# A two-layer SiLU kernel on one core: the first 512 rows computed contraction tile by contraction tile, with x loaded in columns

## The chip, the cores and the metric

The kernel runs on one core of a Trainium2 chip. The metric is device time in microseconds (us), from the kernel's start to its end on that core. A profile is one execution recorded instruction by instruction; its span runs from the first to the last recorded instruction, and the execution's own time is a little longer.

## The reference

```python
x:  (1, 2048, 640) bf16      w1: (640, 1728) bf16      w2: (1728, 640) bf16

h = jnp.einsum("bsd,df->bsf", x, w1)
h = _silu(h)                                   # h * sigmoid(h)
out = jnp.einsum("bsf,fd->bsd", h, w2)
```

So: 2048 rows; a first product that contracts over D = 640, an activation, and a second product that contracts over F = 1728.

## The kernel before

**Tiles.** The 2048 rows are four chunks of SCH = 512 rows (`sc`). D is five contraction tiles of 128 (`dt`), F is thirteen tiles of 128 (`ft`, FR = 13) and a last one of 64. The first product is computed transposed: for one `ft` and one chunk a *unit* (lines 205 to 213) runs five matmuls over `dt` into one of the eight PSUM banks. Each has a 128x128 block of w1 as its loaded weights and 512 columns of the transposed x, `xT_sb[:, dt, cols]`, as the moving operand. `silu` (lines 190 to 203) then lets ScalarE (ACT) write the sigmoid of the bank to `sig_sb` (L193) and VectorE (DVE) multiply the two into `hT_sb` (L196), after which the bank is free. `take_bank` hands the banks out in rotation. The 64 last columns of w1 are done for two chunks at once (`tail_unit`, L219), and the second product follows (L289 and after).

**Order.** A small planner lists operations in program order for each engine, and emits semaphore waits for what each operation depends on. Nothing is reordered: each engine, and each of the two DMA queues in use (SP's and ACT's), runs its list from front to back, and a wait holds up all that stands behind it on that engine.

**The start.** The changed part is the work on the first chunk:

- SP issues rows 0 to 127 and 256 to 383 of x, ACT rows 128 to 255 and 384 to 511, each 128 rows by 640 columns, 160 KB (`load_x0`, L145).
- ACT then issues the first two 128-column pieces of w1, all five contraction tiles of each (`load_w1`, L150). SP waits until its second piece of x has landed, and issues the columns 256 to 511, 512 to 1023 and 1024 to 1727 of w1.
- TensorE (PE) runs six matmuls on constants (L158), five with 512 columns and one with 256, which read nothing that is loaded.
- For each of the four 128-row pieces of x, PE runs five 128x128 transposes (L167) into two banks; DVE copies three of the five to `xT_sb` (L173), ACT the other two (L175).
- `ft` 0 and 1 are computed in two halves of 256 rows each (L209), so that the first two units need only the first two pieces of x. `ft` 2 to 12 take 512 rows a unit.

The transposed x of the other three chunks comes from transposing DMAs (L231), five a chunk, which SP issues after its loads of w1; the first of them waits for the last but one of those loads (`w1_dma[-2]`). Between the second and the third of these chunks SP issues w2 as well. In the rest of the program the order of the work is not touched.

Of the kernel before, what the change touches and what calls it, by code (L numbers as in the profile page):

```python
# [20 lines left out]
class Plan:  # L21
# [9 lines left out]
    def add(self, eng, emit, deps=(), group=None):  # L31
        op = Op(eng, emit, [d for d in deps if d is not None], group)
        self.ops.append(op)
        return op
# [40 lines left out]
def bass_standalone__dense_activation_silu__prompt_kernel(  # L75
# [6 lines left out]
    bf16 = mybir.dt.bfloat16  # L82
# [5 lines left out]
    F = w1.shape[1]  # L88
    P = 128
    H = P // 2  # L90
    SCH = 512
    DT = D // P
    FR = F // P
    F_LAST = F - FR * P
    FT = FR + 1
    ST = S // P
    NSC = S // SCH
    JB = SCH // P
    NBANK = 8
    TPV = 3  # L100
    assert D % P == 0 and S % (2 * SCH) == 0 and F_LAST == H and D == 640

    with ExitStack() as es:
        def sb(name, shape, dtype):
            return es.enter_context(nc.sbuf_tensor(name, shape, dtype))

        xT_sb = sb("xT_sb", [P, DT, S], bf16)
        w1_sb = sb("w1_sb", [P, DT, F], bf16)
# [5 lines left out]
        x0_sb = sb("x0_sb", [P, JB, D], bf16)  # L114
        ident = sb("ident", [P, P], bf16)
        warm_sb = sb("warm_sb", [P, 32], fp32)
        oT_sb = sb("oT_sb", [P, NSC, SCH], bf16)
        ps = es.enter_context(nc.psum_tensor("ps", [P, NBANK, SCH], fp32))

        w1_v = w1.rearrange("(dt p) f -> p dt f", p=P)  # L120
        x0_v = xf[0:SCH, :].rearrange("(j p) d -> p j d", p=P)
# [3 lines left out]
        add = plan.add  # L125
        bank_free = [[] for _ in range(NBANK)]
        turn = [0]

        def take_bank():
            b = turn[0] % NBANK  # L130
            turn[0] += 1
            return b


        XE = 2 * P
        w1_cuts = [0, 1, 2, 4, 8, FT]
        id_a = add("pool", lambda e: e.memset(ident[:, :], 0.0))
        id_b = add("pool", lambda e: e.affine_select(
            out=ident[:, :], in_=ident[:, :], compare_op=ALU.not_equal, fill=1.0,
            base=0, pattern=[[-1, P]], channel_multiplier=1), [id_a])  # L140
        warm = add("dve", lambda e: e.memset(warm_sb[:, :], 0.0))  # L141
        add("act", lambda e: e.activation(out=warm_sb[:, :], in_=warm_sb[:, :], func=ACT.Sigmoid), [warm])  # L142

        def load_x0(eng, j):
            return add(eng, lambda e: e.dma_start(  # L145
                out=x0_sb[:, j, :], in_=x0_v[:, j, :]), group=f"x0_{j}")

        def load_w1(eng, g, deps=()):
            f0, f1 = w1_cuts[g] * P, min(w1_cuts[g + 1] * P, F)
            return add(eng, lambda e: e.dma_start(  # L150
                out=w1_sb[:, :, f0:f1], in_=w1_v[:, :, f0:f1]), deps, group=f"w1_{g}")

        x0_of = [load_x0(eng, j) for j, eng in enumerate(("sp", "act", "sp", "act"))]
        w1_dma = [load_w1("act", 0), load_w1("act", 1)] + [load_w1("sp", g, [x0_of[2]]) for g in (2, 3, 4)]

        ones = nc.const_aps.tensor(1.0, [P, SCH], bf16)
        for n in [SCH] * 5 + [2 * P]:
# [1 line left out]
                ps[:, NBANK - 1, 0:n], lhsT=ones[:, 0:P], rhs=ones[:, 0:n], start=True, stop=True))  # L159

        xT_ready = []
        for j in range(JB):
            cols = slice(j * P, (j + 1) * P)
            ready = []
            for b, d0, d1, eng in ((2 * j, 0, TPV, "dve"), (2 * j + 1, TPV, DT, "act")):
                for dt in range(d0, d1):
                    t = add("pe", lambda e, j=j, b=b, dt=dt, d0=d0: e.transpose(  # L167
                        ps[:, b, :].bitcast(bf16)[:, (dt - d0) * P:(dt - d0 + 1) * P],
                        x0_sb[:, j, dt * P:(dt + 1) * P], ident[:, :]), [x0_of[j], id_b])
                src = ps[:, b, :].bitcast(bf16)[:, 0:(d1 - d0) * P].rearrange("p (k s) -> p k s", s=P)  # L170
                dst = xT_sb[:, d0:d1, cols]
                if eng == "dve":
                    c = add("dve", lambda e, src=src, dst=dst: e.tensor_copy(out=dst, in_=src), [t])  # L173
                else:
                    c = add("act", lambda e, src=src, dst=dst: e.copy(out=dst, in_=src), [t])  # L175
                ready += [c] * (d1 - d0)
                bank_free[b] = [c]
            xT_ready.append(ready)

        def x_deps(sc, c0, n):  # L180
            return xT_ready[(c0 + n) // P - 1] if sc == 0 else [x_dma[sc]]

        def w1_deps(ft):
            return [w1_dma[max(g for g in range(len(w1_dma)) if w1_cuts[g] <= ft)]]

        chunk_done, tail_done = {}, {}
        sig_free = [None] * NSIG
# [2 lines left out]
        def silu(b, parts, n, pe):  # L190
            s = sig_turn[0] % NSIG
            sig_turn[0] += 1
            a = add("act", lambda e: e.activation(  # L193
                out=sig_sb[:, s, 0:n], in_=ps[:, b, 0:n], func=ACT.Sigmoid), [pe, sig_free[s]])
            for rows, ft, cols in parts:
                v = add("dve", lambda e, rows=rows, ft=ft, cols=cols: e.tensor_tensor(  # L196
                    out=hT_sb[rows, ft, cols], in0=ps[rows, b, 0:n], in1=sig_sb[rows, s, 0:n],
                    op=ALU.mult), [a])
                chunk_done[cols.start // SCH] = v
                if ft == FR:  # L200
                    tail_done[cols.start // SCH] = v
            bank_free[b] = [v]
            sig_free[s] = v

        def unit(sc, ft, c0, n):
            b = take_bank()
            cols = slice(sc * SCH + c0, sc * SCH + c0 + n)
            for dt in range(DT):
                pe = add("pe", lambda e, dt=dt: e.matmul(  # L209
                    ps[:, b, 0:n], lhsT=w1_sb[:, dt, ft * P:(ft + 1) * P], rhs=xT_sb[:, dt, cols],  # L210
                    start=(dt == 0), stop=(dt == DT - 1)),
                    x_deps(sc, c0, n) + w1_deps(ft) + bank_free[b] if dt == 0 else ())
            silu(b, [(slice(0, P), ft, cols)], n, pe)

        def tail_unit(sc):
            b = take_bank()
            for dt in range(DT):
                for hh in range(2):
                    pe = add("pe", lambda e, dt=dt, hh=hh: e.matmul(  # L219
                        ps[hh * H:(hh + 1) * H, b, :], lhsT=w1_sb[:, dt, FR * P:F],  # L220
                        rhs=xT_sb[:, dt, (sc + hh) * SCH:(sc + hh + 1) * SCH],
                        start=(dt == 0), stop=(dt == DT - 1), skip_group_check=True),
                        x_deps(sc, 0, SCH) + x_deps(sc + 1, 0, SCH) + w1_deps(FR) + bank_free[b]
                        if dt == 0 else ())
            silu(b, [(slice(hh * H, (hh + 1) * H), FR, slice((sc + hh) * SCH, (sc + hh + 1) * SCH))
                     for hh in range(2)], SCH, pe)

        x_dma, w2_dma = {}, []
        for sc in range(1, NSC):
            for dt in range(DT):  # L230
                x_dma[sc] = add("sp", lambda e, sc=sc, dt=dt: e.dma_start_transpose(  # L231
                    out=xT_sb[:, dt, sc * SCH:(sc + 1) * SCH],
                    in_=xf[sc * SCH:(sc + 1) * SCH, dt * P:(dt + 1) * P]),
                    [w1_dma[-2]], group=f"x{sc}")
            if sc == 2:
                half = FR // 2
                for a, z in ((0, half), (half, FR)):
                    w2_dma.append(add("sp", lambda e, a=a, z=z: e.dma_start(
                        out=w2_sb[:, a:z, :], in_=w2_v[:, a:z, :]), group="w2"))
                for hh in range(2):  # L240
                    w2_dma.append(add("sp", lambda e, hh=hh: e.dma_start(
                        out=w2_sb[hh * H:(hh + 1) * H, FR, :], in_=w2[FR * P:F, :]), group="w2"))

        for ft in range(2):
            for c0 in (0, XE):
                unit(0, ft, c0, XE)
        for ft in range(2, FR):
            unit(0, ft, 0, SCH)

        for sc in range(1, NSC):  # L250
# [114 lines left out]
```

## Time and profile before

| what | us |
|---|---|
| median of three timed runs | 126.41 (126.18, 126.41, 126.73) |
| the profiled execution's own time | 126.71 |
| its span | 125.4 |
| PE busy | 122.2 (97% of the span) |
| DVE busy, ACT busy | 47.6, 41.6 |
| L209, 270 matmuls of the first product | 56.7 |
| L289, second product, all forms | 59.6 |
| granted TensorE clock | 1.00 in all of the span |

How the views are read: a *timeline* lists groups of like instructions by start, each with the stretch from its first start to its last end, the engine, the line, the operands (out<-in) and the count; in brackets stands how long the engine sat idle before it and what released it. PE is the matmul itself, PEld the loading of its weights, SPq and ACTq the issuing of DMAs. *Idle* of an engine is lost time only where nothing else holds the end of the kernel. Matmuls overlap in the pipeline, so their pace is the distance between starts and not the duration of one. The granted clock is what a power throttle allows; it says nothing of the pace at which matmuls start.

When the loads of the first chunk landed in the profiled execution (issue, and time from issue to landing, from the view of DMA issues):

| load | queue | issued | landed after | landed at |
|---|---|---|---|---|
| x rows 0 to 127, 160 KB | SP | 0.73 | 2.5 | 3.2 |
| x rows 128 to 255 | ACT | 0.94 | 2.7 | 3.6 |
| x rows 256 to 383 | SP | 1.2 | 2.8 | 4.0 |
| x rows 384 to 511 | ACT | 1.4 | 3.2 | 4.6 |
| w1 columns 0 to 127, 160 KB | ACT | 1.84 | 3.7 | 5.5 |
| w1 columns 128 to 255 | ACT | 2.33 | 3.8 | 6.1 |
| w1 columns 256 to 511, 320 KB | SP | 4.04 | 4.2 | 8.2 |
| w1 columns 512 to 1023, 640 KB | SP | 4.45 | 5.7 | 10.2 |
| w1 columns 1024 to 1727, 880 KB | SP | 5.04 | 7.4 | 12.4 |

### The profile page before, as it was taken

Reading aid. Unit: us, or ns where it says so; the run is one execution under the profiler, and the core shown is the slowest. Engines: PE = TensorE matmul, PEld = TensorE weight load, DVE = VectorE, ACT = ScalarE, POOL = GpSimd, SP = SyncE. Lnnn points to the kernel's source line nnn. Section 1 sums busy time; section 2 is a strip of 40 time slices with the busy share of each in tenths; the row PEclk is TensorE's granted clock in tenths of the full one; section 3 lists DMA queues with packets and bytes.
Section 4 is the critical chain, followed back from the end, with each engine's and each line's share of the span. In section 5 each row is a group of like instructions: output and inputs, shape, how many; then the busy total and the mean of one; then the engine's idle time right before and its main releaser. Section 6 shows DMA issues by size and latency. Waiting matters only on the chain.

```text
span 125.4 us, 2118 instructions
## 1 busy us (share of the span) xinstructions
PE 122.2 (97%) x910; PEld 58.7 (47%) x910; DVE 47.6 (38%) x74; ACT 41.6 (33%) x73; POOL 0.7 (1%) x6
## 2 busy tenths in 40 slices
PE   7999999999999999999999999999999999999992
PEld 2764444444444444444444444444444444445482
DVE  0454666666666666666664020202020110202022
ACT  4445555555555555555540010101010110101021
POOL 2000000000000000000000000000000000000000
PEclk9999999999999999999999999999999999999999
DMA  4998634489910000000000001113230200112424
GB/s 125 236 314 281 88 85 106 103 251 395 255 43 0 5 0 3 0 0 0 0 0 5 0 0 31 26 21 113 107 110 0 105 0 21 26 22 72 157 80 134
DMA packets 19321, 10.41 MB, mean 83 GB/s; under 512 B 13040, under 2 KB 19312, under 8 KB 19312
## 3 DMA queue, kind: packets, MB, share of 16 engines
q1 hardware_dynamic: 17424, 9.49, 27.0%
q10 hardware_dynamic: 1888, 0.79, 2.3%
q8 instruction: 7, 0.11, 0.4%
q14 instruction: 2, 0.02, 0.0%
HBM read 5.16 MB, written 2.62 MB: 62 GB/s over the span
## 4 chain that ended last, share of the span: by engine, by line
PE 98%; DVE 0%; issue 0%
PE ps L289 47%; PE ps L209 45%; PE ps L158 2%; PE ps L167 2%; PE ps L219 2%; DVE o_sb L300 0%
## 5 line engine op out<-in xcount | busy, mean ns | idle before, releaser
L209 PE MATMUL ps<-xT_sb,w_sb 128*128 128x512 bf16 (+1 forms) x270 | 56.7, 373 | 0.1
L196 DVE TENSOR_TENSOR hT_sb<-ps,sig_sb 128x512 bf16<-128x512 f32 (+2 forms) x58 | 39.1, 673 | 22.3 <-ACT sig_sb L193 21.9
L289 PE MATMUL ps<-w_sb,hT_sb 64*128 64x512 bf16 (+2 forms) x486 | 47.3, 352 | 0.0
L193 ACT ACTIVATE sig_sb<-ps 128x512 bf16<-128x512 f32 (+1 forms) x56 | 32.6, 582 | 26.8 <-PE ps L209 25.7
L209 PEld LDWEIGHTS ps<-xT_sb,w_sb 128*128 128x128 bf16 x270 | 26.4, 98 | 30.2 <-issue 0.4
L289 PEld LDWEIGHTS ps<-w_sb,hT_sb 64*128 64x128 bf16 x486 | 23.3, 94 | 23.7
L300 DVE CAST o_sb<-ps 128x512 bf16<-128x512 f32 (+2 forms) x9 | 5.7, 632 | 37.6 <-PE ps L289 37.6
L302 ACT CAST o_sb<-ps 128x512 bf16<-128x512 f32 (+2 forms) x9 | 4.8, 538 | 38.6 <-PE ps L289 38.6
L289 PE MATMUL ps<-hT_sb,w_sb 64*128 64x512 bf16 x108 | 12.3, 376 | 0.0
L289 PEld LDWEIGHTS ps<-hT_sb,w_sb 64*128 64x128 bf16 x108 | 5.2, 94 | 6.6 <-issue 0.4
L300 DVE CAST oT_sb<-ps 128x512 bf16<-128x512 f32 x2 | 1.4, 691 | 11.7 <-PE ps L289 11.7
L302 ACT CAST oT_sb<-ps 128x512 bf16<-128x512 f32 x2 | 1.2, 586 | 13.6 <-PE ps L289 13.6
L158 PE MATMUL ps<-const-bfloat16-1.0 128*128 128x512 bf16 (+1 forms) x6 | 2.5, 588 | 0.8 <-PEq L350 0.8
L173 DVE COPY xT_sb<-ps 128x384 bf16<-128x384 bf16 x4 | 1.4, 356 | 3.4 <-PE ps L167 3.4
L167 PEld LDWEIGHTS ps<-ident,x_sb 128*128 128x128 bf16 x20 | 2.0, 147 | 0.7 <-DMA x_sb<-in_x_dram 0.7
L219 PE MATMUL ps<-xT_sb,w_sb 128*64 128x512 bf16 x20 | 2.3, 381 | 0.0
L167 PE MATMUL ps<-ident,x_sb 128*128 128x128 bf16 x20 | 2.3, 313 | 0.0
L175 ACT COPY xT_sb<-ps 128x256 bf16<-128x256 bf16 x4 | 1.5, 372 | 2.2 <-PE ps L167 2.2
L219 PEld LDWEIGHTS ps<-xT_sb,w_sb 128*64 128x64 bf16 x20 | 1.0, 110 | 1.2 <-issue 0.4
L158 PEld LDWEIGHTS ps<-const-bfloat16-1.0 128*128 128x128 bf16 x6 | 0.7, 133 | 1.9 <-issue 1.9
L142 ACT ACT_TABLE_LOAD x1 | 1.3, 1283 | 0.7 <-PEq L350 0.7
L141 DVE MEMSET warm_sb<- 128x32 f32 x1 | 0.1, 85 | 0.8 <-PEq L350 0.8
(7 smaller groups left out, 1.1 us busy)
## 6 DMA issues: line engine op xcount, KB each, us to landing
out_dram<-o_sb SPq DMA_DIRECT2D x14, 160.0 KB, 1.9
w_sb<-in_w_dram SPq DMA_DIRECT2D x1, 1120.0 KB, 7.7
w_sb<-in_w_dram SPq DMA_DIRECT2D x1, 960.0 KB, 5.4
w_sb<-in_w_dram SPq DMA_DIRECT2D x1, 880.0 KB, 7.4
w_sb<-in_w_dram SPq DMA_DIRECT2D x1, 640.0 KB, 5.7
x_sb<-in_x_dram SPq DMA_DIRECT2D x2, 160.0 KB, 2.7
x_sb<-in_x_dram ACTq DMA_DIRECT2D x2, 160.0 KB, 2.9
w_sb<-in_w_dram ACTq DMA_DIRECT2D x2, 160.0 KB, 3.8
```

The source lines that it names most:

```text
L142: add("act", lambda e: e.activation(out=warm_sb[:, :], in_=warm_sb[:, :], func=ACT.Sigmoid), [warm])
L158: add("pe", lambda e, n=n: e.matmul(ps[:, NBANK - 1, 0:n], lhsT=ones[:, 0:P], rhs=ones[:, 0:n], start=True, stop=True))
L167: t = add("pe", lambda e, j=j, b=b, dt=dt, d0=d0: e.transpose(ps[:, b, :].bitcast(bf16)[:, (dt - d0) * P:(dt - d0 + 1) * P], x0_sb[:, j, d ...
L173: c = add("dve", lambda e, src=src, dst=dst: e.tensor_copy(out=dst, in_=src), [t])
L175: c = add("act", lambda e, src=src, dst=dst: e.copy(out=dst, in_=src), [t])
L193: a = add("act", lambda e: e.activation(out=sig_sb[:, s, 0:n], in_=ps[:, b, 0:n], func=ACT.Sigmoid), [pe, sig_free[s]])
L196: v = add("dve", lambda e, rows=rows, ft=ft, cols=cols: e.tensor_tensor(out=hT_sb[rows, ft, cols], in0=ps[rows, b, 0:n], in1=sig_sb[rows, ...
L209: pe = add("pe", lambda e, dt=dt: e.matmul(ps[:, b, 0:n], lhsT=w1_sb[:, dt, ft * P:(ft + 1) * P], rhs=xT_sb[:, dt, cols], start=(dt == 0), ...
L219: pe = add("pe", lambda e, dt=dt, hh=hh: e.matmul(ps[hh * H:(hh + 1) * H, b, :], lhsT=w1_sb[:, dt, FR * P:F], rhs=xT_sb[:, dt, (sc + hh) * ...
L289: pe = add("pe", lambda e, b=b, n=n, lhsT=lhsT, rhs=rhs, ft=ft: e.matmul(ps[:, b, 0:n], lhsT=lhsT, rhs=rhs, start=(swap == 0 and ft == 0), ...
L300: ev = add("dve", lambda e, b=b, n=n, dst=dst: e.tensor_copy(out=dst, in_=ps[:, b, 0:n]), [pe])
L302: ev = add("act", lambda e, b=b, n=n, dst=dst: e.copy(out=dst, in_=ps[:, b, 0:n]), [pe])
```

## The change

The first chunk is done contraction tile by contraction tile for the first six `ft`.

- **x** comes in three loads: columns 0 to 255 (`dt` 0 and 1) of rows 0 to 255 on SP and of rows 256 to 511 on ACT, 128 KB each, then columns 256 to 639 of all 512 rows on ACT, 384 KB. ACT's activation that loads its table is put behind its two DMAs.
- **w1**'s first 768 columns come as five loads on SP, one for each contraction tile, 192 KB each. The second of them waits for both of the first loads of x, and all that stands behind it on SP waits with it. Two more loads, columns 768 to 1279 (640 KB) and 1280 to 1727 (560 KB), follow; ACT issues no w1.
- **PE** runs the same six constant matmuls, then the eight transposes of `dt` 0 and 1, then for each `dt` six matmuls of 512 columns, one into each of the six banks 0 to 5. After the groups of `dt` 0, 1 and 2 come the four transposes of `dt` 2, 3 and 4, into the banks 6 and 7 in turn. The copy of a whole contraction tile (128x512) to `xT_sb` is DVE's for even `dt` and ACT's for odd.
- The six units end together in the last group, so that `silu` gets six banks within six matmuls. `ft` 6 to 12 are units as before. There are 260 matmuls of 512 columns on these lines in place of 250, and none of 256 columns in place of 20; the 20 transposes stay.

```diff
-        XE = 2 * P
-        w1_cuts = [0, 1, 2, 4, 8, FT]
+        FA = 6
+        w1_cuts = [FA, 10, FT]
...
+        def load_x0(eng, name, j0, j1, d0, d1):
+            return add(eng, lambda e: e.dma_start(
+                out=x0_sb[:, j0:j1, d0 * P:d1 * P], in_=x0_v[:, j0:j1, d0 * P:d1 * P]), group=name)
+
+        def load_w1(name, d0, d1, f0, f1, deps=()):
+            return add("sp", lambda e: e.dma_start(
+                out=w1_sb[:, d0:d1, f0:f1], in_=w1_v[:, d0:d1, f0:f1]), deps, group=name)
+
+        XA = 2
+        x0_a = [load_x0("sp", "x0_a", 0, JB // 2, 0, XA), load_x0("act", "x0_b", JB // 2, JB, 0, XA)]
+        x0_c = load_x0("act", "x0_c", 0, JB, XA, DT)
         add("act", lambda e: e.activation(out=warm_sb[:, :], in_=warm_sb[:, :], func=ACT.Sigmoid), [warm])
...
-        x0_of = [load_x0(eng, j) for j, eng in enumerate(("sp", "act", "sp", "act"))]
-        w1_dma = [load_w1("act", 0), load_w1("act", 1)] + [load_w1("sp", g, [x0_of[2]]) for g in (2, 3, 4)]
+        w1_lo = [load_w1(f"w1_{dt}", dt, dt + 1, 0, FA * P, x0_a if dt == 1 else ()) for dt in range(DT)]
+        w1_dma = [load_w1(f"w1_{name}", 0, DT, w1_cuts[g] * P, min(w1_cuts[g + 1] * P, F))
+                  for g, name in enumerate("ab")]
...
+        def transpose_x0(dt):
+            b = FA + dt % 2
+            dst = ps[:, b, :].bitcast(bf16)[:, 0:SCH]
+            for j in range(JB):
+                t = add("pe", lambda e, j=j: e.transpose(
+                    dst[:, j * P:(j + 1) * P], x0_sb[:, j, dt * P:(dt + 1) * P], ident[:, :]),
+                    x0_a + [id_b] if dt < XA else [x0_c] + bank_free[b])
+            if dt % 2 == 0:
+                c = add("dve", lambda e: e.tensor_copy(out=xT_sb[:, dt, 0:SCH], in_=dst), [t])
+            else:
+                c = add("act", lambda e: e.copy(out=xT_sb[:, dt, 0:SCH], in_=dst), [t])
+            bank_free[b] = [c]
+            xT_ready.append(c)
...
-        for ft in range(2):
-            for c0 in (0, XE):
-                unit(0, ft, c0, XE)
-        for ft in range(2, FR):
+        for dt in range(XA):
+            transpose_x0(dt)
+        group = [take_bank() for _ in range(FA)]
+        for dt in range(DT):
+            for ft in range(FA):
+                pe = add("pe", lambda e, dt=dt, ft=ft: e.matmul(
+                    ps[:, group[ft], :], lhsT=w1_sb[:, dt, ft * P:(ft + 1) * P], rhs=xT_sb[:, dt, 0:SCH],
+                    start=(dt == 0), stop=(dt == DT - 1)), [xT_ready[dt], w1_lo[dt]] if ft == 0 else ())
+                if dt == DT - 1:
+                    silu(group[ft], [(slice(0, P), ft, slice(0, SCH))], SCH, pe)
+            if dt + XA < DT:
+                transpose_x0(dt + XA)
+        for ft in range(FA, FR):
             unit(0, ft, 0, SCH)
```

More of the change, by code (lines that the diff above doesn't have):

```diff
@@ L141, in bass_standalone__dense_activation_silu__prompt_kernel @@
         warm = add("dve", lambda e: e.memset(warm_sb[:, :], 0.0))
-        add("act", lambda e: e.activation(out=warm_sb[:, :], in_=warm_sb[:, :], func=ACT.Sigmoid), [warm])
[L144 to L151, printed above, removed]
-        x0_of = [load_x0(eng, j) for j, eng in enumerate(("sp", "act", "sp", "act"))]
-        w1_dma = [load_w1("act", 0), load_w1("act", 1)] + [load_w1("sp", g, [x0_of[2]]) for g in (2, 3, 4)]
+        def load_x0(eng, name, j0, j1, d0, d1):
[7 more added lines that the diff above has]
+        x0_c = load_x0("act", "x0_c", 0, JB, XA, DT)
+        add("act", lambda e: e.activation(out=warm_sb[:, :], in_=warm_sb[:, :], func=ACT.Sigmoid), [warm])
+        w1_lo = [load_w1(f"w1_{dt}", dt, dt + 1, 0, FA * P, x0_a if dt == 1 else ()) for dt in range(DT)]
+        w1_dma = [load_w1(f"w1_{name}", 0, DT, w1_cuts[g] * P, min(w1_cuts[g + 1] * P, F))
+                  for g, name in enumerate("ab")]
         ones = nc.const_aps.tensor(1.0, [P, SCH], bf16)
@@ L161, in bass_standalone__dense_activation_silu__prompt_kernel @@
         xT_ready = []
[L162 to L178, printed above, removed]
+        def transpose_x0(dt):
[11 more added lines that the diff above has]
+            xT_ready.append(c)
         def x_deps(sc, c0, n):
-            return xT_ready[(c0 + n) // P - 1] if sc == 0 else [x_dma[sc]]
+            return xT_ready if sc == 0 else [x_dma[sc]]
         def w1_deps(ft):
-            return [w1_dma[max(g for g in range(len(w1_dma)) if w1_cuts[g] <= ft)]]
+            return [w1_dma[max(g for g in range(len(w1_dma)) if w1_cuts[g] <= ft)]] if ft >= FA else w1_lo
         chunk_done, tail_done = {}, {}
```

## Prediction

> **What bounds the kernel.** I read the chain of work that ended last first, in order of time.
>
> ```profile
> 0.77 2.50 PE ps L158 x6
> 3.28 2.30 PE ps L167 x20
> 5.58 0.13 issue
> 5.71 56.70 PE ps L209 x270
> 62.41 2.28 PE ps L219 x20
> 64.69 58.47 PE ps L289 x594
> ```
>
> The columns are start, length, engine and line. PE holds the end from 0.77 us on. The change can only win or lose in three ways: PE idle before the last L209 matmul, the pace of PE, and what follows if a load or a bank comes too late. Next, the timeline of the start.
>
> ```profile
> 3.26 2.05 PEld L167 LDWEIGHTS ps<-ident,x_sb 128*128 128x128 bf16 x20 [0.68 <-DMA x_sb<-in_x_dram]
> 3.26 2.31 PE L167 MATMUL ps<-ident,x_sb 128*128 128x128 bf16 x20
> 3.80 0.36 DVE L173 COPY xT_sb<-ps 128x384 bf16<-128x384 bf16 x1 [2.90 <-PE ps L167]
> ...
> 4.33 0.36 DVE L173 COPY xT_sb<-ps 128x384 bf16<-128x384 bf16 x1 [0.18 <-PE ps L167]
> ...
> 5.68 0.35 PEld L209 LDWEIGHTS ps<-xT_sb,w_sb 128*128 128x128 bf16 x3 [0.37 <-issue]
> ```
>
> DVE's copies start 0.53 apart, once every five transposes, so a transpose starts every 0.107 us. The transposes begin with the first piece of x (landed 3.23) and are never late again. The last starts at 5.26, so PE has nothing new from 5.37 to 5.71; the first w1 piece lands at 5.54. Then the timeline a little later:
>
> ```profile
> 6.77 0.38 ACT L193 ACTIVATE sig_sb<-ps 128x256 bf16<-128x256 f32 x1 [0.79 <-PE ps L209]
> 7.32 0.38 ACT L193 ACTIVATE sig_sb<-ps 128x256 bf16<-128x256 f32 x1 [0.16 <-PE ps L209]
> ...
> 8.28 7.67 PEld L209 LDWEIGHTS ps<-xT_sb,w_sb 128*128 128x128 bf16 x37 [0.19 <-DMA w_sb<-in_w_dram]
> ```
>
> The sigmoids follow every 0.545 us, five 256-column matmuls, 0.109 each. But cut into slices of 0.01 us the timeline has the first L209 matmuls start at 5.71, 5.88, 6.09, 6.30, 6.46, 6.57: some 0.21 apart, and from about **6.40** on 0.11. The constant matmuls of 512 columns also start 0.427 apart, and later ones 0.216 (a sigmoid every 1.08 us for five). So PE works at half pace from 0.77 until 6.40, though the granted clock is 1.00 in every slice. The last line shows the only load that PE waits for after its start: 0.19 us.
>
> **What follows for the sum.** Before 6.40 an idle microsecond costs only half of one, since the work put off runs later at double pace. So I count, at 6.40, what each kernel still owes at full pace.
>
> *Before* has done about 3.5 matmuls of 256 columns by then, that is 1.75 of 512, and all transposes.
>
> *After, first transpose.* It needs two loads of 128 KB, one per queue, in rows of 512 bytes. The nearest rows are 160 KB loads in rows of 1280 bytes that landed 2.5 us (SP) and 2.7 us (ACT) after issue. ACT's DMA no longer stands behind the table load and goes out near 0.75 in place of 0.94. That makes 3.2 to 3.5; I take 3.43, and 3.2 to 4.0 for the range, the latter if shorter rows cost as much as the third load of x did.
>
> *After, first matmul.* The fourth transpose starts 0.32 later and takes 0.314: 4.07. The DVE copy is 512 wide; by the 384-wide row, 0.356 x 512/384 = 0.475, so 4.55. Its w1 tile (192 KB, second on SP, issued near 1.16) lands at 4.0 if it takes the 2.8 of the second SP load before, at 4.9 if it takes the 3.7 of ACT's w1 load. I take a start at **4.6**, bounds 4.3 and 4.9. Until 6.40 that gives 1.8/0.427 = 4.2 matmuls: 2.45 more than before, worth 2.45 x 0.216 = **-0.53**.
>
> *Twelve transposes are still owed* (`dt` 2 to 4). No row shows one at full pace. Upper bound: the 0.107 of now, 1.28. Lower bound: half of it, 0.64. Weight loads took 0.147 under L167 and 0.098 under L209; scaled by that, 0.071 each, which I take as the row of the same step: **+0.86**.
>
> *The stall of 0.19* at 8.28 goes, **-0.19**, if no other load is late. Ten matmuls fewer: 20 x 0.109 - 10 x 0.216 = **-0.02**.
>
> *Loads.* x and the first w1 tile are 852 kB. Before, 175 GB/s in 0.77 to 3.28 and 234 GB/s in 3.28 to 5.71 moved 1.0 MB by 5.71; at that pace the last columns of x land by 5.1, and the transposes that need them come after six matmuls, at 6.8. SP's wait for both first loads replaces one for the second; behind it queue the other four w1 tiles, the two larger loads and every transposing DMA. It ends near 3.45 rather than 4.04. With issues of 0.39 to 0.67 us each and, as in 6.40 to 8.28, 326 GB/s, the four tiles land near 5.9, 6.5, 7.1 and 7.7, wanted at 7.1, 8.7, 10.2 and 11.5; columns 768 up land near 9.7, wanted at 12.8. This cover of 1.1 us or more prices them at nothing. The next chunk's transposing DMAs started at 10.20, when w1's fourth load had landed, and the fifth landed near 19.5 for a use near 20.0. Now they start no later, with 560 KB of w1 in flight rather than 880; if they slipped by a whole microsecond, half a microsecond would show.
>
> *The six activations at once.* ACT needs 0.60 a tile, DVE 0.69, so the last of six is done some 4 us after the group. PE has two free banks, 2.16 us of work, and wants bank 0 then; its product is done some 0.5 us after the group, and DVE frees one every 0.69 against PE's 1.08. Nothing is late. The copies of `dt` 1 to 4 have a group of six matmuls (1.3 us) as cover against 0.48 on DVE and, by ACT's 0.585 for 512 columns, 0.59 there.
>
> *Switches.* PE now goes three times more from matmuls to transposes and back. The one switch on record had PE empty for 0.34 us, of which the load's landing at 5.54 explains all but some 0.1. I take 0; the other end is 3 x 0.34 = 1.0.
>
> Sum: -0.53 + 0.86 - 0.19 - 0.02 = **+0.12 us**. On the profiled execution's 126.71 that is 126.83; that execution lies 0.30 above the median of the three runs, so on the median's 126.41 it is **126.5**, my forecast. Within the bounds (start 4.3 to 4.9, transposes 0.64 to 1.28) it is 126.2 to 127.1.
>
> **A rule against the trace.** The trace's change of pace at 6.40 came after 2.3 us of transposes and 0.7 us of matmuls. The Trainium skill, "TensorE: Matmul & The Clock Gate" (Part 4: PE-mode transpose), says that transposes do not count as busy for the gate that halves the pace. If so, matmuls that begin 1.1 us sooner would end the slow pace about as much sooner, half of it gained: -0.55, and 126.0. The row speaks against it, since there mostly transposes preceded the change. Part 1 of the same page has the gate judge windows of about 3.4 us that start at no fixed point of the kernel; no view here shows a window, but by it the 6.40 would differ from run to run in both kernels.
>
> **Rivals.**
>
> 1. *The slow pace lasts longer (slower, 0.20).* PE was empty for only 0.5 us between 0.77 and 6.40. Now a gap opens ahead of the transposes (to 3.43) and one while DVE copies (4.29 to 4.6). If PE must be busy without such gaps and starts afresh at 4.6, the 5.6 us from 0.77 to 6.40 end at 10.2: (10.2 - 6.4)/2 = 1.9 us more, 128.4. For it: the gap lies in the stretch before 6.40. Against: 0.34 us empty before 5.71 did no such harm. It decides once the gap is longer than the monitor forgives, which no row shows.
> 2. *Each switch costs (slower, 0.18).* If the 0.34 us is PE emptying itself between a transpose and a matmul, three more make +1.0, with the return +2.0; 127.5 to 128.5. For it: the chain calls the gap "issue", not DMA. Against: the load landed within it.
> 3. *The full pace comes with the matmuls (faster, 0.17).* At best at 4.6: (6.4 - 4.6)/2 = 0.9 us less, 125.6. For it: real matmuls start 1.1 us sooner than before. Against: the change of pace fell 0.7 us after the first real matmul, and could have come sooner.
> 4. *The loads do not arrive by contraction tile as intended*, because all share the same stretch of near-full DMA (0.94 busy in 3.28 to 5.71). Then the first matmul comes at 5.5 rather than 4.6, +0.45 at half price: 127.0, still no difference to speak of. Chance 0.05.
>
> **The numbers.** A measurement of this kernel tells about 0.5% (0.63 us) from no change. Forecast 0.40 and rival 4 0.05 give "same" 0.45; rivals 1 and 2 give "slower" 0.38; rival 3 "faster" 0.17. The range reaches from rival 3's 125.6 to 128.2, which takes in switches at +1.0 and most of their dearer form and leaves out the full price of rival 1.
>
> **What would show it.** First L209-type group near 4.6 and 0.427 apart; starts 0.216 apart from about 6.4, later under rival 1, before 5.5 under rival 3; transposes of `dt` 2 to 4 at 0.05 to 0.11 with no PE gap round them (rival 2: gaps of 0.3); no wait for w1 after that; the first-product matmuls end near 62.5 in a like execution. I am wrong if the change of pace moves by more than 1.3 us, or if a group waits for its w1 tile.

## The result, and the profile after

| | before | changed |
|---|---|---|
| median, seven runs each | 126.35 us | 127.47 us |
| lowest | 126.18 | 126.88 |
| profiled execution, its span | 126.71, 125.4 | 127.62, 126.2 |

The ratio changed to before is **1.0079, interval 1.0052 to 1.0105**: about 1.0 us slower. Medians here and below are over all runs, while ratios leave out the runs more than 1.5% above the fastest of their kernel (five of twelve in run 2, four of twelve in run 9, at most one elsewhere), so the two need not agree.

The chain of the changed kernel (start, length, engine and line) is the view that differs most. Before, PE alone held the end from 0.77 us on. Now:

```profile
5.31 6.31 DMA w_sb<-in_w_dram
11.62 0.02 issue
11.64 1.21 SPq L231
...
16.79 4.13 DMA xT_sb<-in_x_dram
20.93 0.05 issue
20.97 1.90 PE ps L209 x8
...
63.23 2.28 PE ps L219 x20
65.51 58.47 PE ps L298 x594
```

A load of w1 lands at 11.62, SP then issues the five transposing DMAs of the second chunk, the fifth lands at 20.93, and only then does PE go on. Everything behind, from L219, lasts as long as before (58.47 for the second product) and begins 0.82 us later, at 63.23 in place of 62.41. The timeline of PE at that place, with the idle time ahead in brackets:

```profile
20.97 0.55 PEld L209 LDWEIGHTS ps<-xT_sb,w_sb 128*128 128x128 bf16 x4 [1.96 <-DMA xT_sb<-in_x_dram]
20.97 0.82 PE L209 MATMUL ps<-xT_sb,w_sb 128*128 128x512 bf16 x3 [1.47 <-DMA xT_sb<-in_x_dram]
```

Matmuls start 0.216 apart, and with nothing to wait for the second chunk's first one would have started at some 19.3: a stall of about 1.6 us. If 1.6 us are lost there and only 0.8 at the end, the start itself must have won 0.8. Its timeline:

```profile
3.53 1.01 PE L170 MATMUL ps<-ident,x_sb 128*128 128x128 bf16 x8 [0.25 <-DMA x_sb<-in_x_dram]
4.15 0.42 DVE L174 COPY xT_sb<-ps 128x512 bf16<-128x512 bf16 x1 [3.25 <-PE ps L170]
...
4.63 1.47 PE L249 MATMUL ps<-xT_sb,w_sb 128*128 128x512 bf16 x6
...
5.94 0.39 PE L170 MATMUL ps<-ident,x_sb 128*128 128x128 bf16 x4
...
6.16 1.46 PE L249 MATMUL ps<-xT_sb,w_sb 128*128 128x512 bf16 x6
```

Six matmuls from 4.63 and four transposes from 5.94 to 6.16: by single starts the first six are 0.21 to 0.23 apart and the four transposes 0.055. In this execution PE was at full pace from its first real matmul, where before it got there only at 6.40. So two things moved, against each other: when PE gets to full pace, and when the second chunk's x lands.

### The profile page after: what moved, and what is told of

The parts are those of the page before. It is cut to its first block, busy times and chain, and to the rows that moved or that the text cites. A ratio compares the mean times of both kernels' runs of the same rounds, so it can differ in the third digit from the quotient of the medians.

```text
span 126.2 us, 2089 instructions
## 1 busy us (share of the span) xinstructions
PE 121.1 (96%) x895; PEld 57.0 (45%) x900; DVE 46.3 (37%) x71; ACT 40.2 (32%) x69; POOL 0.7 (1%) x6
## 4 chain that ended last, share of the span: by engine, by line
PE 81%; DMA 10%; SPq 5%; issue 1%; DVE 0%
PE ps L298 46%; PE ps L209 33%; DMA w_sb<-in_w_dram 5%; SPq L231 4%; DMA xT_sb<-in_x_dram 3%; DMA x_sb<-in_x_dram 2%; PE ps L219 2%; SPq L148 1%; DVE o_sb L309 0%; SPq L64 0%
## 5 line engine op out<-in xcount | busy, mean ns | idle before, releaser
L209 PE MATMUL ps<-xT_sb,w_sb 128*128 128x512 bf16 x226 | 49.8, 379 | 1.7 <-DMA xT_sb<-in_x_dram 1.5
L196 DVE TENSOR_TENSOR hT_sb<-ps,sig_sb 128x512 bf16<-128x512 f32 (+1 forms) x56 | 37.9, 690 | 20.3 <-ACT sig_sb L193 20.2
L193 ACT ACTIVATE sig_sb<-ps 128x512 bf16<-128x512 f32 x54 | 31.5, 601 | 26.2 <-PE ps L209 22.4
L209 PEld LDWEIGHTS ps<-xT_sb,w_sb 128*128 128x128 bf16 x230 | 22.4, 98 | 28.9 <-DMA xT_sb<-in_x_dram 2.0
L249 PE MATMUL ps<-xT_sb,w_sb 128*128 128x512 bf16 x29 | 7.1, 379 | 0.1
L174 DVE COPY xT_sb<-ps 128x512 bf16<-128x512 bf16 x3 | 1.3, 425 | 7.7 <-PE ps L170 7.7
L249 PEld LDWEIGHTS ps<-xT_sb,w_sb 128*128 128x128 bf16 x30 | 2.7, 98 | 2.9 <-DVE xT_sb L174 0.4
L176 ACT COPY xT_sb<-ps 128x512 bf16<-128x512 bf16 x2 | 1.2, 586 | 4.0 <-PE ps L170 4.0
L219 PE MATMUL ps<-xT_sb,w_sb 128*64 128x512 bf16 x20 | 2.3, 381 | 0.0
L219 PEld LDWEIGHTS ps<-xT_sb,w_sb 128*64 128x64 bf16 x20 | 1.0, 110 | 1.2 <-issue 0.4
```

The costliest lines, as they stand in the source:

```text
L193: a = add("act", lambda e: e.activation(out=sig_sb[:, s, 0:n], in_=ps[:, b, 0:n], func=ACT.Sigmoid), [pe, sig_free[s]])
L209: pe = add("pe", lambda e, dt=dt: e.matmul(ps[:, b, 0:n], lhsT=w1_sb[:, dt, ft * P:(ft + 1) * P], rhs=xT_sb[:, dt, cols], start=(dt == 0), ...
L219: pe = add("pe", lambda e, dt=dt, hh=hh: e.matmul(ps[hh * H:(hh + 1) * H, b, :], lhsT=w1_sb[:, dt, FR * P:F], rhs=xT_sb[:, dt, (sc + hh) * ...
L249: pe = add("pe", lambda e, dt=dt, ft=ft: e.matmul(ps[:, group[ft], :], lhsT=w1_sb[:, dt, ft * P:(ft + 1) * P], rhs=xT_sb[:, dt, 0:SCH], st ...
```

## The experiments

Theory A: the transposing DMAs now wait for a load that ends later, and that wait is the loss. Its rival B: the queue is simply full, and they would land late however early they were issued. Later two more: C, the moment of full pace differs by execution and hangs on how steadily PE was busy, and the reordered start is more exposed to it; D, that moment is mere chance, or the spread is that of the loads. "Step" below is the moment at which the distance between starts halves.

### 1. The changed kernel, waiting for an earlier load

```diff
-                    [w1_dma[-2]], group=f"x{sc}")
+                    [w1_lo[-1]], group=f"x{sc}")
```

> The changed kernel, but the second chunk's transposing DMAs wait for the last of the five w1 tiles (landed near 8.4 in the profile after) and not for columns 768 to 1279 (11.6). Theory A, the wait moved onto a later load is the whole loss and the start itself won: the transposing DMAs begin some 3.2 us sooner, the 1.6 us in which PE waits for x at 20.97 go, and the time is 127.5 - 1.6 = about 125.9, below the kernel before. Theory B, the queue is what is full: the transposing DMAs begin sooner but stand behind 1.2 MB of w1 on the same queue, land when they did (near 20.9), and the time stays near 127.5. In between if they land near 19.5.

Median 126.74; ratio to before 1.0025 (0.9997 to 1.0052). Its chain:

```profile
12.11 9.28 PE ps L209 x43
21.39 0.05 issue
21.45 10.74 PE ps L209 x49
...
61.75 2.28 PE ps L219 x20
```

No DMA stands between the first chunk and the second: SP issued the DMAs from 8.93, the fifth landed near 16.9. A holds and B falls. The profiled execution took 126.06, as A said, the fastest of the twelve, and L219 starts 0.66 us *sooner* than before. But over the runs only about half a per cent came back (1.0079 to 1.0025, 0.7 us), not 1.6 us. In its profile the step is at 4.9. Something else differs between executions, which led to C and D.

### 2. The changed kernel, cut where the old one was

```diff
-        w1_cuts = [FA, 10, FT]
+        w1_cuts = [FA, 8, FT]
```

> The changed kernel, but the first of the two larger w1 loads ends at column 1023, as the load waited for in the kernel before did; the wait stays on that load. Theory A: 328 kB less to land before the wait ends, some 1.0 us at 326 GB/s, so the transposing DMAs begin near 10.6, PE's wait shrinks from 1.6 to about 0.6 us, and the time is about 126.5. Theory B: no difference, 127.5.

```profile
5.29 5.27 DMA w_sb<-in_w_dram
10.56 0.02 issue
10.57 1.20 SPq L231
...
15.72 4.30 DMA xT_sb<-in_x_dram
20.02 0.05 issue
20.07 1.90 PE ps L209 x8
...
62.33 2.28 PE ps L219 x20
```

In this chain the wait ends 1.07 us sooner, the second chunk starts 0.90 sooner and L219 starts 0.90 sooner (62.33 against 63.23), as A had it. The ratio is 1.0021 (0.9989 to 1.0053), but it rests on seven of the twelve runs; the median of all twelve is 127.3, where A said 126.5. So the chain shows the shift, and the times alone do not settle it.

### 3 and 4. The kernel before, waiting for a later or an earlier load

```diff
-                    [w1_dma[-2]], group=f"x{sc}")
+                    [w1_dma[-1]], group=f"x{sc}")      # run 3;  [w1_dma[-3]] in run 4
```

> The kernel before, with the second chunk's transposing DMAs waiting for the last w1 load (landed 12.4) and not for the one ahead of it (10.2). Theory A: 2.2 us later; the fifth landed near 19.2 for a use near 20.0, so about 1.4 us of wait at PE and about 127.8, with nothing else changed. Theory B: the queue is empty by then, so the transposing DMAs run faster and make up for most of it: under 127.0.

> The kernel before, with the transposing DMAs waiting for the columns 256 to 511 (landed 8.2) in place of 10.2. Theory A: no change, 126.35, since PE did not wait for them before. Its profile also gives one more execution of the old start, for the moment at which the matmuls go to full pace: near 6.4 again if the order of the work sets it, anywhere between 4.5 and 7.5 if it is chance.

Later: 127.19, ratio 1.0055 (1.0029 to 1.0082). The wait alone makes the old kernel slower, with no other edit. It cost half of what A said: issued from 12.32, the fifth DMA landed at 20.50, 8.2 us after the first issue against 8.9 before, with less w1 in flight beside it; whether that is a part for B is not shown. Earlier: 126.24, ratio 0.9987 (0.9962 to 1.0012), no change, as A said. The steps in these two profiles of the old start: between 4.2 and 5.0, and 3.7. It was 6.4 in the first profile.

### 5 and 6. More and fewer constant matmuls, transposing DMAs early

Run 5 fills PE's two gaps, run 6 widens the first. Both start from experiment 1.

```diff
-        for n in [SCH] * 5 + [2 * P]:
+        for n in [SCH] * 6 + [P]:                      # run 5;  [SCH] * 2 + [2 * P] in run 6
...
         group = [take_bank() for _ in range(FA)]
+        add("pe", lambda e: e.matmul(                  # run 5 only
+            ps[:, FA - 1, 0:2 * P], lhsT=ones[:, 0:P], rhs=ones[:, 0:2 * P], start=True, stop=True))
```

> The kernel of the first experiment (transposing DMAs no longer late), with more constant matmuls in PE's two gaps: the last 256 columns ahead of the transposes become 512 and 128, and 256 columns stand between the eight transposes and the first group. They cost nothing if PE would have been empty. Four starts in the profiles so far went to full pace at 3.7, 4.1 to 4.9, 4.3 to 4.7 and 6.4, so the moment differs by execution. Theory C, the moment hangs on how steadily PE was busy: the filled start goes to full pace sooner, the runs well above the rest (127.8 and 128.6 against 126.1 to 127.2 in the first experiment) become rarer and the median falls by 0.3 to 0.6 us to about 126.2. Theory D, the moment is chance that PE's gaps do not touch, or the spread is that of the loads: median near 126.7, within 0.2, and the same spread.

> The kernel of the first experiment with three constant matmuls (two of 512 columns and one of 256) in place of six, so that PE is empty from about 1.8 to 3.5 us ahead of the transposes. No load and no other instruction is changed. Theory C: the pace steps up some 1 to 2 us later in most executions, the median rises by 0.5 to 1.7 us to 127.2 or more, and many runs lie near 128.5. Theory D: no change, 126.7.

Filled: 126.43, highest 126.98, ratio 1.0009 (0.9989 to 1.0030). Fewer: 127.61, lowest 127.36, ratio **1.0110** (1.0077 to 1.0144). Not one load was touched, so D falls for run 6. For run 5 the median fell by 0.3, and the intervals of the two ratios overlap; the gain from filling is likely, not settled. The timeline of run 6:

```profile
3.74 1.01 PE L170 MATMUL ps<-ident,x_sb 128*128 128x128 bf16 x8 [1.74 <-DMA x_sb<-in_x_dram]
4.84 2.74 PE L249 MATMUL ps<-xT_sb,w_sb 128*128 128x512 bf16 x6
7.38 0.48 PE L170 MATMUL ps<-ident,x_sb 128*128 128x128 bf16 x4
7.69 1.46 PE L249 MATMUL ps<-xT_sb,w_sb 128*128 128x512 bf16 x6
```

PE idles 1.74 us ahead of its transposes; the first group of six then takes 2.74 (0.427 apart), the next, after a step at about 7.55, 1.46. In run 5 it took 1.85, with the step at 5.56. That is later than in run 1 (4.9), so the one profile of run 5 does not show the earlier step that C forecast; the gain is seen in the times alone. Run 6 took PE work away as well as widening the gap, and no run tells these two apart.

### 7 and 10. The same two edits on the changed kernel as it is

> The changed kernel, still with its late transposing DMAs, and the same two fillers. Theory A says that PE waits for x near 20.9 whatever the start did, so an earlier full pace is lost in that wait: near 127.4, no gain over the changed kernel except that its runs near 129 go. If the start counted by itself it would gain as much as the filler does without the wait.

> The changed kernel, late transposing DMAs and all, with three constant matmuls in place of six. With the DMAs early, that edit made the pace step up at 7.5 and cost 0.87 us in the medians. Theory A with C: PE then comes to the second chunk near 20.8 in place of 19.3, and x lands near 20.9 anyway, so the two losses overlap and the time hardly moves: 127.4 to 127.9 against 127.5. Rival: the losses have nothing to do with each other and add up, 128.3.

Filled: 127.21, ratio 1.0072 (1.0045 to 1.0099): no gain over 1.0079, as A said. Fewer: 128.38, ratio 1.0151 (1.0127 to 1.0174): the expectation that the two losses overlap **missed**, and the rival's 128.3 was met. Yet in the profiled execution (128.03) they did not add up. The chain of run 10 shows no DMA between the chunks at all:

```profile
4.72 2.74 PE ps L249 x6
7.46 0.43 PE ps L170 x4
7.89 1.87 PE ps L249 x6
...
63.73 2.28 PE ps L219 x20
```

Its second group is still slow (1.87), the step came at 8.9. The late start had used up the wait (matmuls start 0.216 apart right through the place, and only the weight load idled, 0.2 us) and went past it. Why the step is later there than in run 6 (7.55), with the same work on PE, I cannot say from one profile each. In the profile of run 7 the w1 load landed at 10.9, not 11.6, and the fifth transposing DMA at 19.36, not 20.93; the weight load waited 0.4 us, the matmuls lost 0.03, and that execution took 126.08, the fastest of its ten. So the loads differ by execution too, and the wait with them.

### 8. The kernel before with three constants

```diff
-        for n in [SCH] * 5 + [2 * P]:
+        for n in [SCH] * 2 + [2 * P]:
```

> The kernel before with three constant matmuls in place of six. Theory C: its first matmul comes at 5.5 to 5.7, when the first w1 piece lands, whatever the pace of the transposes, so a pace that steps up later costs it only from there on: less than it costs the reordered start, some 0.3 to 1.2 us, 126.7 to 127.5. Theory D: no change, 126.4.

Median 127.07, ratio 1.0067 (1.0033 to 1.0101); in the profile the step is at 7.5. The old start is exposed as well, by 0.7% where the reordered one lost 0.85% (1.0025 to 1.0110); the intervals do not tell these two apart.

### 9 and 11. Two attempts at a faster version

Run 9 starts from run 5, takes the contraction tiles 2 to 4 of the first chunk through transposing DMAs, and lets ACT issue w1's tiles, behind its table load and with no wait between them (the cut below leaves these last edits out):

```diff
+        x0_t = {dt: add("sp", lambda e, dt=dt: e.dma_start_transpose(
+            out=xT_sb[:, dt, 0:SCH], in_=xf[0:SCH, dt * P:(dt + 1) * P]), group=f"x0t{dt}") for dt in range(XA, DT)}
...
-            if dt + XA < DT:
-                transpose_x0(dt + XA)
```

> A version that takes up what the runs showed: transposing DMAs of the second chunk early, gaps filled with constants, and the contraction tiles 2 to 4 of the first chunk transposed by DMA (SP, right after its first load of x) and not by PE, so that the third load of x, 12 transposes and three copies go; w1's tiles are issued by ACT with no wait. PE's twelve transposes at 0.055 each are 0.66 us. If the DMAs land in time (tiles wanted near 7.7, 9.0 and 10.3; issued 1.2 to 5.0, landing 2.7 to 4.4 later as others did) the time is 126.4 - 0.7 = about 125.8, below the kernel before. The rival: the transposing DMAs, which took 1.2 to 2.1 us of SP each, slow the other loads at the start or hold back columns 768 up behind them, a group waits for its tile, and the time is 126.5 or more.

> The kernel before with the transposing DMAs early (as in the fourth experiment) and w1's first two pieces of 128 columns loaded as one of 256, so in rows of 512 bytes and not 256. The old start is bound by the first piece's landing near 5.5. If short rows are what makes it late, the one load lands near 5.3 and the first matmul comes up to 0.2 us sooner: 126.1 to 126.3 against 126.36, at most just below the kernel before. If twice the bytes cost more than the longer rows gain, it lands near 6 and the time is 126.5 to 126.8.

Run 9: median 128.43, ratio 1.0054 (1.0011 to 1.0097). The time is the rival's, and a load at the start was late:

```profile
1.40 4.62 DMA w_sb<-in_w_dram
6.02 0.14 issue
6.15 8.08 PE ps L253 x30
```

The first w1 tile landed 4.62 us after its issue, at 6.02 (at 4.38 in the changed kernel), the first matmul came at 6.15, and the step at about 9.1. After that no group waited. Whether the transposing DMAs or the move to ACT's queue made the tile late, no run tells. Run 11 (the kernel before with `w1_cuts = [0, 2, 4, 8, FT]` and the early wait of run 4): 126.83, ratio 1.0041 (1.0024 to 1.0058). The one load of 256 columns landed 3.7 us after issue, at 5.57, where the 128 columns landed before, yet the version is slower. In its profile the step is at 6.40 again and L219 starts at 62.31, where it was 62.41 before, so the one execution profiled does not show what the runs lost; that stays open. No version beat the kernel before: the best were run 4 and run 5, equal to it.

## Why the prediction was right and wrong

The forecast was 126.5 us, no change. The kernel lost 1.0 us, inside the range but on the side of "slower", and not by either of the rivals that I had put there. That it came so close is luck: in the profiled execution a gain of 0.8 us that the sum did not have met a loss of 1.6 that it did not have either. By the prediction's own sign it was wrong, since the change of pace moved by more than 1.3 us (from 6.40 to 4.63 or sooner).

**The step that failed** is the one on loads: "Now they start no later", with columns 768 up landing "near 9.7". They landed at 11.62, and the transposing DMAs started at 11.64 where before it was 10.20. The sum took a load to be there when the bytes up to its end had moved. Two rows of the windows of each kernel, from the start of the span, say otherwise. In a row stand the stretch, the busy time of the engines, granted clock, DMA share and, last, GB/s. Before:

```profile
0.00:8.90 8.90, 7.99 (x49) 5.13 (x50) 2.85 (x9) 4.53 (x10) 0.70 (x6) 1.00 0.79 220
0.00:10.19 10.19, 9.28 (x55) 5.72 (x56) 3.20 (x9) 5.13 (x11) 0.70 (x6) 1.00 0.81 236
```

Changed:

```profile
0.00:9.70 9.70, 8.59 (x47) 4.24 (x48) 1.24 (x4) 2.69 (x4) 0.70 (x6) 1.00 0.77 234
0.00:11.62 11.62, 10.46 (x55) 5.05 (x56) 1.44 (x5) 3.40 (x6) 0.70 (x6) 1.00 0.77 242
```

The first chunk of x and w1 up to column 1279 are 2.29 MB; with the rest of w1 it is 2.87. In the changed kernel 2.27 MB had moved by 9.70, so the sum had the bytes right. But the load that the wait names landed only when 2.81 MB had moved, nearly all of the load issued behind it too: the two went side by side. The kernel before shows the same: 1.97 MB reach up to column 1023, 1.96 had moved by 8.90, and that load landed at 10.19 with 2.4 MB moved. So the prediction set a landing reckoned by bytes, 9.7, against one measured, 10.20. Reckoned alike, the old wait ends at 8.9 and the new one, 328 kB further on, 0.8 later; measured, it ended 1.4 later.

The stretch from first issue to fifth landing was 8.9 us before and 9.3 after, so the later start went through whole: the fifth landed at 20.93 in place of 19.14 (the prediction read 19.5). I had even priced it, as half a microsecond if they slipped by one. The landing slipped by 1.8 against a margin of 1.0 (the second chunk began at 20.16 before), and PE came 0.8 sooner: 1.6 us of stall.

**The sum at 6.40, term by term, in the profiled execution.** First transpose 3.53 (3.43 taken), first matmul 4.63 (4.6 taken): held. Twelve transposes: 0.055 each, 0.66 us, near the lower bound of 0.64; I had 0.86, scaled by the weight loads, and the pace of matmul starts was the better scale. The stall of 0.19 on w1 went, but it was too dear: 0.19 is the idle time of the weight load, while matmuls that had been starting 0.11 apart start at 8.10 and 8.28, so 0.08 was lost. Column 768 landed at 11.62 for a matmul that started at 11.79, so the cover of "1.1 us or more" was nearly nothing there. Switches: 0 as taken; rival 2 is refuted by the timeline above, where four transposes fill exactly 0.22 us between two groups.

**The step fixed at 6.40** was the larger mistake of method: I took one execution's moment as a property of the kernel. The starts that share the old order of loads and PE work had it at 6.40, at 4.2 to 5.0, at 3.7 and at 6.40 again (the kernel before, runs 3, 4 and 11). In the changed kernel's profile it came no later than the first matmul, the moment that rival 3 named, and its 0.9 us are there: 0.8 won ahead of the stall. That the matmuls bring it is not shown: in run 4 it came amid transposes, in run 5 0.8 us after the first real matmul. Rival 1 exists too: with PE idle for 1.6 to 1.7 us (runs 6 and 10), or starved by its loads (run 9), the step came at 7.55, 8.9 and 9.1. Where PE never waits for a load after its first matmul, L219 starts as follows:

| reordered start | step | L219 starts |
|---|---|---|
| run 1 | 4.9 | 61.75 |
| run 5 | 5.6 | 62.08 |
| run 6 | 7.55 | 63.13 |

From the first to the last, 1.38 us over 2.65: half a microsecond for each that the step is late, as the prediction's rule said. The old order had 62.01 at 3.7 (run 4), 62.41 at 6.4 and 62.82 at 7.5 (run 8): 0.15 a microsecond up to 6.4, since until some 5.5 PE waits for the first piece of w1 whatever its pace, and 0.4 beyond. In run 4 PE, so early at full pace, also came 0.23 us too soon for the columns 512 to 1023 of w1; its chain:

```profile
4.53 5.45 DMA w_sb<-in_w_dram
9.99 0.05 issue
10.03 9.45 PE ps L209 x43
```

So, in these profiles, the reordered start wins with an early step (61.75 against 62.01, nearly all of it by that wait) and loses with a late one (63.13 at 7.55 against 62.82 at 7.5). Over the runs the two come out even: 1.0025 and, with the gaps filled, 1.0009.

**Why the step moves** is open. The steps of the old start lie 2.7 us apart between executions of like work. The Trainium skill, "TensorE: Matmul & The Clock Gate" (Part 1: The HAM clock gate), says that the gate looks at windows which do not begin with the kernel, so that the moment varies; that agrees, while its half a microsecond of variation is too little here. The same page's Part 4 (PE-mode transpose) has transposes not count as busy in the same way as matmuls: run 4 went to full pace at 3.7 amid transposes, after constants that ended at 3.1, which neither shows nor refutes it.

**What is shown and what is not.** Shown: the late DMAs cost most of it (0.7 us of 1.0). With only the wait changed, the ratio goes from 1.0079 to 1.0025 (the changed kernel and run 1, intervals that just touch) and, with the gaps filled, from 1.0072 to 1.0009 (runs 7 and 5, intervals apart); and a later wait slows the old kernel by itself. Shown: fewer constants, and nothing else, cost 0.85%. Argued only: that what run 1 does not win back (0.25% over the kernel before, in an interval that holds zero) is the step falling later in its other executions than in the profiled one. The timed runs without a profile have no trace, so their steps were not seen.

## What to carry to other kernels

When a load is recut, follow every wait that names it by its place in a list: `w1_dma[-2]` still named the last but one load, but that load now ended 256 columns later, and the transfers behind the wait decided the time ten microseconds on. An order of work that starts the real matmuls sooner gains only as much as PE's pace at that moment allows; read that pace from the distances between starts in several executions before a single moment is put into a sum. And a gain ahead of a transfer that lands at a fixed time is only a longer wait.

## What the runs showed of the hardware

- The distance between 512-column matmuls (or its counterpart for 256 columns and for transposes) went from 0.427 to 0.216 us at a moment between 3.7 and 9.1 us in thirteen profiles, with a granted clock of 1.00 in each. With no gap of a microsecond in PE's work from 0.77 on: 3.7 to 6.4 (nine profiles). With PE idle for 1.5 us or more in all ahead of its first real matmul, by the distances between starts: 7.5 to 9.1 (runs 6, 8, 9 and 10; in runs 8 and 9 in two pieces).
- A 128x128 transpose starts every 0.107 us at half pace and every 0.055 at full, and goes between groups of matmuls without a gap.
- A transposing DMA of 512x128 held SP for 1.2 us, now and then for 1.5 to 2.4. The five of the second chunk landed 2.5 to 5.4 us after issue; the three that run 9 issued beside the first loads took 5.0 to 7.5, and its first tile of w1 landed 1.6 us later than in the changed kernel.
- Loads issued one behind the other on SP's queue moved side by side: one of 640 KB landed 1.3 us (before) and 1.9 us (changed) after the bytes up to its end had moved.
